# Attention and a gated layer in one kernel: another order at the attention's group boundaries, in its first group, and of the token blocks

## The chip, the cores and the metric

The kernel runs on one core of one Trainium2 chip. The metric is the device time of one execution in microseconds (us), less is better. The engines of a core are PE (matrix products; PEld is its loading of weights, which runs beside the products), DVE (element-wise work), ACT (functions such as tanh and exp), POOL (element-wise work, little used here) and SP (here it issues the transfers). Each engine works through its own list of instructions in order; between engines an instruction waits for semaphores.

## The reference

Attention over 4 batches of 12 heads with 448 tokens of 64 elements, with scores that are capped by a tanh, and then a layer with a cosine gate on the 1792 tokens, all in float32:

```python
scores = cap * np.tanh((q @ k.T / sqrt(64)) / cap)         # per batch and head
scores = scores - scores.max(axis=-1)
attn = np.exp(scores); attn = attn / attn.sum(axis=-1)
x = (attn @ v)                                             # joined over heads: 1792 x 768
h = x @ w_in                                               # 768 -> 2048
return (h * np.cos(h)) @ w_out                             # 2048 -> 768
```

With a cap below a limit, as here, exp needs no maximum and the kernel leaves it out.

## The kernel before, in words

**Attention.** The 48 pairs of a batch and a head are worked in NO = 6 groups of eight; groups n = 0 to 2 hold batches 0 and 1, groups 3 to 5 batches 2 and 3. A group has NC = 7 chunks c of 64 keys, and each chunk two halves a of four pairs. A *unit* j is one half of one chunk: PE computes its scores (`scores`, L293, 8 matmuls into one of two PSUM banks of tag `pair`, each of which the trace shows as two records), and ACT takes the tanh of 128x896 values from the bank into half of a tile `t` (`tanh`, L312). Two units are one *step* (42 in all): ACT then takes exp in place over the whole 128x1792 tile (`exp`, L319). There are four `t` tiles, so the tanh of step i waits until all that reads the tile of step i-4 is done: on DVE the addition of the chunk into the running sum over chunks (`add`, L358, for c = 1 to 5), on PE the product with v (`values`, L376, 16 matmuls of a step into two banks `acc`).

At the end of a group, PE sums over the keys with a matrix of ones, once over the last chunk and once over DVE's running sum (`sums`, L387); the result z takes one of the two `pair` banks too. DVE then makes the result's parts, a chain of nine instructions: transpose (`norm_sums`, L406), reciprocal, transpose, two products of `acc` with the reciprocals into x0 and x1 (`norm_scale`, L423), two copies to the high parts xh (`norm_high`, L428) and two subtractions for the low parts xl (`norm_low`, L431). The first addition of the next group stood behind all nine.

**Order of the work.** `attention` (L448) writes the order out by hand: `at(step, time, call)` puts every call on one list with the key STEP * step + time, and the list is sorted and emitted in that order. Only the order counts; what an engine does first is what comes first on the list. The two weights of 64-bit words are turned into float parts on the way (a *piece* of a weight: one ACT instruction `magnitude`, L197, and six DVE instructions), at the steps of the table DECODE (L37).

**First group.** `unit(j)` (L246) gives the order in which halves and chunks of group 0 are taken: (a, c) = (0,0), (0,1), (1,0), (1,1), (0,2), (0,3), (1,2), (1,3), and then both halves of each chunk. Its chunks 0 and 1 both come due for `values` in step 3, ahead of the scores of step 4.

**The layer.** The tokens are worked in four blocks (BLOCKS, L26), the 2048 hidden columns in 8 groups G of 2x128. One step (`Layers.step`, L679) is one block of one G: PE makes h of both columns (`hidden`, L155, 36 matmuls), then the product with w_out for the block of the step before (`Block.product`, L606, 36 matmuls), while ACT and DVE make the gate. `begin(0)` and `begin(1)` (L649) make h of block 0 already in the attention's last steps. The banks `single` that take h of block 1 are the space that `acc` held, so the first of them waits until `norm_scale` of group 5 has read it.

Of the kernel before, what the change touches and what calls it, by code (L numbers as in the profile page):

```python
# [10 lines left out]
F32 = mybir.dt.float32  # L11
# [3 lines left out]
AF = mybir.ActivationFunctionType  # L15
# [7 lines left out]
DM = H * D  # L23
DFF = 2048
KC = DM // 128
BLOCKS = 512, 512, 384, 384  # L26
STARTS = 0, 512, 1024, 1408
WIDE = max(BLOCKS)
NF = DFF // 128
NQUAD = NPAIR // 2  # L30
# [3 lines left out]
ND = NJ // 2  # L34
DIRECT = 1
STEP = 3.4
DECODE = [(7, 10, 11, 12, 13, 14), (17, 18, 19, 20, 21, 24), (26, 27, 28, 31, 32, 33), (35, 38, 39, 40)]  # L37
BUSY = 8, 3
PAD = 80
QK = 2 * S  # L40
# [204 lines left out]

def unit(j):  # L246
    n, i = divmod(j, 2 * NC)
    if n or i > 7:
        return n, i % 2, i // 2
    return 0, i // 2 % 2, 2 * (i // 4) + i % 2  # L250


WHERE = {unit(j): j for j in range(NJ)}
# [2 lines left out]
class Heads:  # L256


    def __init__(self, ctx, tc, banks, qk, v, capt, inv, xh, xl, bounded):
        nc = tc.nc  # L260
        self.nc, self.qk_in, self.v_in, self.capt, self.inv = nc, qk, v, capt, inv
        if bounded:
            self.inv, self.capt = in_register(nc, inv, "inv"), in_register(nc, capt, "cap")
        self.cap_column = capt
        self.xh, self.xl, self.bounded = xh, xl, bounded
        cp = ctx.enter_context(tc.tile_pool(name="a_const", bufs=1))
        self.ld = ctx.enter_context(tc.tile_pool(name="a_ld", bufs=8 if bounded else 4))
# [8 lines left out]
        self.qk, self.v, self.ps, self.ts, self.left = {}, {}, {}, {}, {}  # L276
        self.sum, self.acc, self.x, self.z, self.r, self.s = {}, {}, {}, {}, {}, {}

    def fill(self):
# [32 lines left out]
    def tanh(self, j):  # L312
        i, k = divmod(j, 2)
        if k == 0:
            self.ts[i] = self.tp.tile([128, 2, 2, S], F32, name="t", tag="t")
            self.left[i] = 2
        self.nc.scalar.activation(self.ts[i][:, k], self.ps.pop(j)[:, :, 0:S], AF.Tanh, scale=self.inv)  # L317

    def exp(self, i):  # L319
        self.nc.scalar.activation(self.ts[i], self.ts[i], AF.Exp, scale=self.capt)  # L320

    def t(self, n, a, c):
        j = WHERE[n, a, c]
        return self.ts[j // 2][:, j % 2]

    def used(self, n, c):
        for a in range(2):
            i = WHERE[n, a, c] // 2
            self.left[i] -= 1
            if not self.left[i]:  # L330
                del self.ts[i]

    def exp_general(self, n):
        nc, ident = self.nc, self.ident
# [112 lines left out]
def attention(ctx, tc, banks, busy, second, qk, v, capt, inv, xh, xl, wts, layers):  # L447
# [7 lines left out]
    def at(step, time, call, *args):  # L455
        todo.append((STEP * step + time, len(todo), call, args))
# [15 lines left out]
    for n in range(NO):  # L472
        begin = NC * n
        for c in range(NC):
            at(begin - 2 * NC + 2 + c if n > 1 else n - 1, 0.3 + 0.1 * c, a.load_v, n, c)
        for p in range(4):
            if n:
                at(begin - NC + (-1, 2, 3, 4)[p] if n > 1 else -0.5, 0.8, a.load, n, p // 2, p % 2)
        for c in range(NC):
            i = max(WHERE[n, p, c] for p in range(2)) // 2 + 2  # L480
            lag = 1 if c < NC - 1 and 0 < n and (n, c) not in ((NO - 1, NC - 3), (NO - 1, NC - 2)) else 0
            if c == NC - 1:
                at(i, 0.3, a.sums, n, c)
                at(i, 0.4, a.sums, n, None)
            for e in range(2):
                at(i + lag, (0.5, 0.7)[e] if c == NC - 1 else 0.1, a.values, n, c, e)
            if 0 < c < NC - 1:
                at(i, 0.15, a.add, n, c)
            if c:
                at(i + lag, 0.75 if c == NC - 1 else 0.18, a.used, n, c)  # L490
            if c == 1:
                at(i + lag, 0.19, a.used, n, 0)
        for m, (part, args) in enumerate([("sums", ()), ("inverse", ()), ("spread", ()), ("scale", (0,)), ("scale", (1,)),
                                          ("high", (0,)), ("high", (1,)), ("low", (0,)), ("low", (1,))]):
            at(i, 1.0 + 0.1 * m, getattr(a, "norm_" + part), n, *args)
    pieces = (("wi", 0), ("wi", 1), ("wo", 0), ("wo", 1), ("wi", 2))
    at(5, 3.3, wts.load, *pieces[0])
    for n, steps in enumerate(DECODE):
# [1 line left out]
                 (wts.high, *pieces[n], nc.vector), (wts.low, *pieces[n], nc.vector)]  # L500
        at(steps[0] - 1, 3.3, wts.magnitude)
        for step, call in zip(steps, calls):
            at(step, 2.5, *call)
        at(steps[3], 2.6, wts.load, *pieces[n + 1])
    at(ND - 1, 1.7, layers.begin, 0)
    at(ND, 1.65, layers.sine)
    at(ND, 1.7, layers.first, second)
    at(ND + 1, 0.3, layers.begin, 1)
    for _, _, call, args in sorted(todo, key=lambda x: x[:2]):
        call(*args)  # L510

# [281 lines left out]
```

## Time and profile before

| | us |
|---|---|
| median of 3 runs (648.32 to 651.06) | 649.91 |
| the profiled execution | 649.24 |
| its span, first to last instruction | 647.4 |
| PE busy in the span | 620.4 (96%) |
| DVE busy | 488.0 (75%) |
| ACT busy | 306.5 (47%) |
| POOL busy | 54.7 (8%) |

The span has two parts with different limits, so its shares are means over both. In the chain of work that ended last, from the span's start to about 185 us PE, ACT and DVE take turns (attention); from there on it is PE alone (the layer). PE's time printed per instruction includes the filling of its pipeline, so neighbouring instructions overlap in the table; from when one starts to when the next starts is the better measure.

### The profile page before, as it was taken

To read this page: it belongs to the slowest core of one execution; us is meant where nothing else is said; L and a number is where in the kernel's file an instruction comes from. 1 tells how busy PE (TensorE), PEld (TensorE's weight loads), DVE (VectorE), ACT (ScalarE), POOL (GpSimd) and SP (SyncE) were. 2 spreads that over 40 slices of the span, in tenths; PEclk is the share of its full clock that TensorE was granted. 3 is DMA by queue.
4 is the path that set the end of the run, shared out by engine and by line. 5 is a ranking of instruction groups with operands and counts; after the bars stand their busy time and mean duration, and the time that the engine had idled before them with its cause. 6 is when DMAs were issued, how large, how long until landed. Compare 5 with 4: busy or idle time off the path is not lost.

```text
span 647.4 us, 11991 instructions
## 1 busy us (share of the span) xinstructions
PE 620.4 (96%) x5207; PEld 470.7 (73%) x5207; DVE 488.0 (75%) x643; ACT 306.5 (47%) x383; POOL 54.7 (8%) x36
## 2 busy tenths in 40 slices
PE   8988898988879999999999999999999999999996
PEld 2323242322458998898899889889988998998896
DVE  1567868778578888777887898788789877877654
ACT  6889897897613343333334333343343333333220
POOL 0000000000011111111111111111111111111000
PEclk9999899999989999999999999999999999999999
DMA  7625243320101112111111221111111221110224
GB/s 230 226 58 177 86 147 121 113 79 2 51 0 51 49 54 94 49 50 50 49 50 50 60 84 52 50 50 49 50 50 49 81 67 49 50 49 1 100 97 152
DMA packets 22782, 48.06 MB, mean 74 GB/s; under 512 B 2496, under 2 KB 9920, under 8 KB 22720
## 3 DMA queue, kind: packets, MB, share of 16 engines
q1 hardware_dynamic: 22576, 47.00, 22.1%
q8 instruction: 43, 0.70, 0.4%
q10 hardware_dynamic: 144, 0.20, 0.1%
q14 instruction: 19, 0.16, 0.1%
HBM read 41.68 MB, written 5.51 MB: 73 GB/s over the span
## 4 chain that ended last, share of the span: by engine, by line
PE 85%; DVE 9%; ACT 4%; issue 1%; DVEq 0%; ACTq 0%
PE single L162 35%; PE pair L619 24%; PE rest L619 12%; PE pair L303 6%; PE acc L381 5%; ACT t L317 2%; DVE x L423 2%; DVE sum L365 2%; DVE xl L431 2%; PE pair L395 1%; PE pair L162 1%; DVE s L406 1%; DVE s L419 1%; ACT t L320 1%; DVE xh L428 1%
## 5 line engine op out<-in xcount | busy, mean ns | idle before, releaser
L582 ACT ACTIVATE y<-y,angles 128x384 f32<-128x384 f32 (+1 forms) x63 | 42.3, 671 | 120.3 <-DVE y L579 120.3
L303 PE MATMUL pair<-qk 64*32 64x448 f32 x1232 | 74.9, 554 | 14.3 <-ACT t L317 14.3
L317 ACT ACTIVATE t<-pair 128x896 f32<-128x896 f32 x84 | 74.3, 935 | 24.1 <-DVE sum L365 16.6
L381 PE MATMUL acc<-t,v 64*32 64x448 f32 x1344 | 77.4, 539 | 0.4 <-DVE x L423 0.2
L320 ACT ACTIVATE t<-t 128x1792 f32<-128x1792 f32 x42 | 72.3, 1725 | 0.0
L632 DVE TENSOR_TENSOR acc<-pair,acc 128x1024 f32<-128x1024 f32 (+1 forms) x56 | 60.8, 1086 | 10.5 <-PE pair L619 10.5
L570 ACT ACTIVATE v<-single,angles 128x384 f32<-128x384 f32 (+1 forms) x62 | 39.1, 630 | 57.2 <-PE single L162 57.1
L303 PEld LDWEIGHTS pair<-qk 64*32 64x32 f32 x1232 | 20.0, 106 | 60.1 <-ACT t L317 47.6
L588 ACT CAST gh<-y 128x384 fp32r<-128x384 f32 (+1 forms) x63 | 35.7, 567 | 51.0 <-DVE y L585 51.0
L381 PEld LDWEIGHTS acc<-t,v 64*32 64x32 f32 x1344 | 26.9, 107 | 40.7 <-issue 29.0
L591 DVE TENSOR_TENSOR gl<-y,gh 128x384 fp32r<-128x384 f32 (+1 forms) x63 | 54.1, 859 | 2.5 <-ACT gh L588 2.5
L197 ACT ACTIVATE u<-w 128x768 f32<-128x768 f32 x32 | 29.2, 912 | 55.1 <-POOL wo2l L230 10.0
L573 DVE TENSOR_SCALAR v<-v 128x384 f32<-128x384 f32 (+1 forms) x63 | 24.6, 390 | 32.4 <-ACT v L570 32.4
L365 DVE TENSOR_TENSOR sum<-sum,t 128x1792 f32<-128x1792 f32 x20 | 40.5, 2025 | 8.8 <-ACT t L320 8.5
L579 DVE SCALAR_TENSOR_TENSOR y<-v,y 128x384 f32<-128x384 f32 (+1 forms) x63 | 39.3, 624 | 2.2
L585 DVE TENSOR_TENSOR y<-single,y 128x384 f32<-128x384 f32 (+1 forms) x62 | 38.3, 617 | 3.2 <-ACT y L582 3.2
L578 DVE SCALAR_TENSOR_TENSOR y<-v,single 128x384 f32<-128x384 f32 (+1 forms) x62 | 38.4, 619 | 2.1
L212 DVE TENSOR_SCALAR u<-u 128x768 f32<-128x768 f32 x32 | 17.7, 554 | 27.7 <-ACT u L197 27.6
L162 PE MATMUL single<-xh,wi0h 128*128 128x384 f32 (+1 forms) x90 | 33.2, 369 | 3.5 <-DVE x L423 3.5
L162 PE MATMUL single<-xh,wi2l 128*128 128x512 f32 (+1 forms) x96 | 35.0, 364 | 0.0
L162 PE MATMUL single<-xh,wi2h 128*128 128x512 f32 (+1 forms) x96 | 34.9, 364 | 0.0
L619 PE MATMUL pair<-gh,wo0l 128*128 128x512 f32 (+1 forms) x96 | 34.8, 363 | 0.0
(153 smaller groups left out, 1461.9 us busy)
## 6 DMA issues: line engine op xcount, KB each, us to landing
w<-in_w_in_dram SPq DMA_DIRECT2D x32, 384.0 KB, 3.6
w<-in_w_out_dram SPq DMA_DIRECT2D x32, 384.0 KB, 3.5
qk<-in_qk_dram SPq DMA_DIRECT2D x20, 448.0 KB, 3.5
v<-in_v_dram SPq DMA_DIRECT2D x42, 128.0 KB, 2.5
out_dram<-acc SPq DMA_DIRECT2D x6, 512.0 KB, 2.7
out_dram<-acc SPq DMA_DIRECT2D x5, 384.0 KB, 3.1
qk<-in_qk_dram SPq DMA_DIRECT2D x2, 288.0 KB, 2.9
qk<-in_qk_dram SPq DMA_DIRECT2D x2, 160.0 KB, 3.6
```

The costliest lines, as they stand in the source:

```text
L162: nc.tensor.matmul(h[:, 0:n], lhsT=w[:, ks], rhs=x[:, k, toks], start=(k == 0 and i == 0), stop=(k == KC - 1 and i == 2))
L303: self.nc.tensor.matmul(ps[o:o + 32, h, 0:S], lhsT=x[mine, k:k + 32], rhs=x[mine, Q], start=True, stop=True, tile_position=(64 * h, o))
L317: self.nc.scalar.activation(self.ts[i][:, k], self.ps.pop(j)[:, :, 0:S], AF.Tanh, scale=self.inv)
L320: self.nc.scalar.activation(self.ts[i], self.ts[i], AF.Exp, scale=self.capt)
L365: self.nc.vector.tensor_add(out, old, self.ts[NC * n + c])
L381: self.nc.tensor.matmul(self.acc[n, e][o, r], lhsT=self.v[n, c][rows, d], rhs=self.t(n, a, c)[rows, h], start=c == 0, stop=c == NC - 1, ti ...
L570: m.nc.scalar.activation(self.v, self.h, AF.Identity, bias=m.quarter, scale=1.0 / (2.0 * math.pi))
L579: m.nc.vector.scalar_tensor_tensor(self.y, self.v, -TWO_PI_LO, self.y, op0=ALU.mult, op1=ALU.add)
L582: self.m.nc.scalar.activation(self.y, self.y, AF.Sin, bias=self.m.half_pi)
L591: self.m.nc.vector.tensor_sub(self.result(1), self.y, self.result(0))
L619: m.nc.tensor.matmul((y[e] if self.last(i) else y[:, e])[:, 0:n], lhsT=w[:, c], rhs=x[:, j, 0:n], start=(j == 0 and k == 0), stop=(j == GF ...
L632: m.nc.vector.tensor_add(acc, y[:, e, 0:n], acc)
```

## The change

Five edits, all of them in the order, apart from the first step's buffers:

1. *At a boundary on DVE*: the first addition of the new group comes right behind the two products `norm_scale`; the two `norm_high` follow it, and the two `norm_low` wait until the end of the new group, ahead of its first transpose.
2. *At a boundary on PE*: both `sums` come ahead of the next group's next eight score matmuls (keys 0.15 and 0.16 in place of 0.3 and 0.4; the scores have 0.2). `begin(1)` moves behind the last `sums` and `values`.
3. *First group*: only the first four units have the other order; the tiles of step 0 are x0 and x1, which are free until the first `norm_scale`, so exp of that step is two instructions of 128x896; `values` of chunks 0 and 1 stand apart, one half of chunk 0 ahead of the scores, the rest between and behind them.
4. *Token blocks*: 512, 384, 512, 384 in place of 512, 512, 384, 384. Block 1 then lies in batches 0 and 1.
5. *Weights and loads*: another table DECODE; loads of v two steps later.

```diff
-BLOCKS = 512, 512, 384, 384
-STARTS = 0, 512, 1024, 1408
+BLOCKS = 512, 384, 512, 384
+STARTS = 0, 512, 896, 1408
...
-DECODE = [(7, 10, 11, 12, 13, 14), (17, 18, 19, 20, 21, 24), (26, 27, 28, 31, 32, 33), (35, 38, 39, 40)]
+DECODE = [(8, 8, 8, 8, 11, 12), (13, 14, 18, 19, 20, 21), (25, 25, 26, 27, 28, 32), (33, 35, 39, 40)]
...
 def unit(j):
     n, i = divmod(j, 2 * NC)
-    if n or i > 7:
+    if n or i > 3:
         return n, i % 2, i // 2
-    return 0, i // 2 % 2, 2 * (i // 4) + i % 2
+    return 0, i // 2, i % 2
...
         if k == 0:
-            self.ts[i] = self.tp.tile([128, 2, 2, S], F32, name="t", tag="t")
+            if i or not self.bounded:
+                t = self.ts[i] = self.tp.tile([128, 2, 2, S], F32, name="t", tag="t")
+                self.half[i] = [t[:, 0], t[:, 1]]
+            else:
+                self.half[i] = [self.np.tile([128, 2, S], F32, name=f"x{e}", tag=f"x{e}") for e in range(2)]
...
-        self.nc.scalar.activation(self.ts[i], self.ts[i], AF.Exp, scale=self.capt)
+        for t in [self.ts[i]] if i else self.half[i]:
+            self.nc.scalar.activation(t, t, AF.Exp, scale=self.capt)
...
-            at(begin - 2 * NC + 2 + c if n > 1 else n - 1, 0.3 + 0.1 * c, a.load_v, n, c)
+            at(begin - 2 * NC + 4 + c if n > 1 else n - 1, 0.3 + 0.1 * c, a.load_v, n, c)
...
             if c == NC - 1:
-                at(i, 0.3, a.sums, n, c)
-                at(i, 0.4, a.sums, n, None)
+                at(i, 0.15, a.sums, n, c)
+                at(i, 0.16, a.sums, n, None)
             for e in range(2):
-                at(i + lag, (0.5, 0.7)[e] if c == NC - 1 else 0.1, a.values, n, c, e)
+                time = (0.5, 0.7) if c == NC - 1 else (0.1, 2.0) if i == 3 and c == 0 else (2.5, 2.51) if i == 3 else (0.1, 0.1)
+                at(i + lag, time[e], a.values, n, c, e)
...
-        for m, (part, args) in enumerate([("sums", ()), ("inverse", ()), ("spread", ()), ("scale", (0,)), ("scale", (1,)),
-                                          ("high", (0,)), ("high", (1,)), ("low", (0,)), ("low", (1,))]):
+        for m, (part, args) in enumerate([("sums", ()), ("inverse", ()), ("spread", ()), ("scale", (0,)), ("scale", (1,))]):
             at(i, 1.0 + 0.1 * m, getattr(a, "norm_" + part), n, *args)
+        for e in range(2):
+            at(i + 2, 0.5, a.norm_high, n, e)
+            at(i + NC if n < NO - 1 else i + 2, 0.9, a.norm_low, n, e)
...
-    at(ND + 1, 0.3, layers.begin, 1)
+    at(ND + 1, 0.9, layers.begin, 1)
```

DVE at the boundary from group 3 to group 4, before (`u`, `wo0h` are a weight's pieces, `s` and `r` the reciprocals on their way, `sum` the running sum):

```order
L218 SCALAR_TENSOR_TENSOR u<-w_77,u 128x768
L406 STREAM_TRANSPOSE s<-pair 128x896
L413 RECIPROCAL r<-s 128x28
L419 STREAM_TRANSPOSE s<-r 128x896
L423 TENSOR_TENSOR x_1572<-acc,s 128x896
L423 TENSOR_TENSOR x_1574<-acc,s 128x896
L428 CAST xh<-x_1572 128x896
L428 CAST xh<-x_1574 128x896
L431 TENSOR_TENSOR xl<-x_1572,xh 128x896
L431 TENSOR_TENSOR xl<-x_1574,xh 128x896
L365 TENSOR_TENSOR sum<-t 128x1792
```

The same place on DVE now (lines are numbered anew; L371 is the addition, L412 the first transpose, L437 the low parts):

```order
L215 TENSOR_SCALAR u<-u 128x768
L437 TENSOR_TENSOR xl<-x_1240,xh 128x896
L437 TENSOR_TENSOR xl<-x_1242,xh 128x896
L412 STREAM_TRANSPOSE s<-pair 128x896
L419 RECIPROCAL r<-s 128x28
L425 STREAM_TRANSPOSE s<-r 128x896
L429 TENSOR_TENSOR x_1574<-acc,s 128x896
L429 TENSOR_TENSOR x_1576<-acc,s 128x896
L371 TENSOR_TENSOR sum<-t 128x1792
L434 CAST xh<-x_1574 128x896
L434 CAST xh<-x_1576 128x896
```

The addition has moved up past four instructions; the low parts that stand ahead of the transpose are those of the group before, x_1240 and x_1242.

PE at a boundary before (L303 scores, L395 sums, L381 values):

```order
L381 MATMUL acc<-t,v 32x448 x16
L303 MATMUL pair<-qk 32x448 x8
L395 MATMUL pair<-t,one 32x448 x8
L395 MATMUL pair<-sum,one 32x448 x8
L381 MATMUL acc<-t,v 32x448 x8
L303 MATMUL pair<-qk 32x448 x8
```

PE at a boundary now (L401 sums, L387 values):

```order
L387 MATMUL acc<-t,v 32x448 x16
L401 MATMUL pair<-t,one 32x448 x8
L401 MATMUL pair<-sum,one 32x448 x8
L303 MATMUL pair<-qk 32x448 x8
L387 MATMUL acc<-t,v 32x448 x8
L303 MATMUL pair<-qk 32x448 x8
```

Sums and the first eight scores have changed places. z so takes the `pair` bank ahead of them, and the second eight scores get the bank that z held.

DVE at the end of attention, before (`second` is the gate of the layer's first unit):

```order
L579 SCALAR_TENSOR_TENSOR second<-second 128x512
L585 TENSOR_TENSOR second<-pair,second 128x512
L406 STREAM_TRANSPOSE s<-pair 128x896
L413 RECIPROCAL r<-s 128x28
L419 STREAM_TRANSPOSE s<-r 128x896
```

And now:

```order
L588 SCALAR_TENSOR_TENSOR second<-second 128x512
L594 TENSOR_TENSOR second<-pair,second 128x512
L437 TENSOR_TENSOR xl<-x_1892,xh 128x896
L437 TENSOR_TENSOR xl<-x_1894,xh 128x896
L412 STREAM_TRANSPOSE s<-pair 128x896
```

Here too the two low parts of the group before have come in between the gate and the last group's chain.

## Rows read from the trace of the kernel before

**Rows 1.** Windows: length, busy (count) of PE, PEld, DVE, ACT, POOL; clock, DMA, GB/s

```profile
6.85:49.31 42.46, 38.27 (x700) 13.00 (x684) 20.79 (x22) 35.22 (x34) 0.00 (x0) 1.00 0.54 175
49.31:157.73 108.42, 98.55 (x1920) 34.30 (x1920) 82.89 (x75) 93.42 (x87) 0.00 (x0) 0.98 0.34 108
185.45:189.08 3.63, 3.63 (x10) 2.80 (x11) 3.02 (x4) 0.52 (x1) 0.00 (x0) 0.57 0.00 0
303.39:361.19 57.80, 57.80 (x289) 52.06 (x289) 47.75 (x68) 21.09 (x33) 7.39 (x4) 1.00 0.17 55
```

**Rows 2.** Waits of ACT, 5 to 170 us: total, times, longest

```profile
ACT t L317 <- DVE sum L365: 16.6, 5, 3.5
ACT t L317 <- PE pair L303: 7.5, 10, 2.8
```

**Rows 3.** Waits of PE's weight loads, 5 to 170 us

```profile
PEld pair L303 <- ACT t L317: 49.1, 53, 2.8
```

**Rows 4.** ACT timeline, boundary of groups 3 and 4: start, length, ..., [idle before <-releaser]

```profile
125.39 1.70 ACT L320 ACTIVATE t<-t 128x1792 f32<-128x1792 f32 x1
130.47 1.73 ACT L317 ACTIVATE t<-pair 128x896 f32<-128x896 f32 x2 [3.38 <-DVE sum L365]
...
133.67 1.73 ACT L317 ACTIVATE t<-pair 128x896 f32<-128x896 f32 x2
```

**Rows 5.** DVE timeline, the same boundary

```profile
113.87 2.02 DVE L365 TENSOR_TENSOR sum<-sum,t 128x1792 f32<-128x1792 f32 x1 [0.70 <-ACT t L320]
115.82 0.99 DVE L218 SCALAR_TENSOR_TENSOR u<-w,u 128x768 int32<-128x768 int32 x1
120.55 1.12 DVE L406 STREAM_TRANSPOSE s<-pair 128x896 f32<-128x896 f32 x1 [3.74 <-PE pair L395]
...
123.28 2.09 DVE L423 TENSOR_TENSOR x<-acc,s 128x896 f32<-128x896 f32 x2
125.28 1.16 DVE L428 CAST xh<-x 128x896 fp32r<-128x896 f32 x2
126.35 2.09 DVE L431 TENSOR_TENSOR xl<-x,xh 128x896 fp32r<-128x896 f32 x2
128.35 2.02 DVE L365 TENSOR_TENSOR sum<-t 128x1792 f32<-128x1792 f32 x1
```

**Rows 6.** PE timeline, the same boundary

```profile
118.71 0.99 PE L395 MATMUL pair<-t,one 64*32 64x448 f32 x16
119.48 0.96 PE L395 MATMUL pair<-sum,one 64*32 64x448 f32 x16
...
126.20 1.71 PE L303 MATMUL pair<-qk 64*32 64x448 f32 x32
127.70 1.72 PE L381 MATMUL acc<-t,v 64*32 64x448 f32 x32
```

**Rows 7.** ACT timeline, first group

```profile
19.89 1.73 ACT L317 ACTIVATE t<-pair 128x896 f32<-128x896 f32 x2 [0.96 <-PE pair L303]
...
27.36 1.73 ACT L317 ACTIVATE t<-pair 128x896 f32<-128x896 f32 x2 [0.96 <-PE pair L303]
```

**Rows 8.** DVE timeline, end of attention

```profile
174.44 0.69 DVE L585 TENSOR_TENSOR second<-pair,second 128x512 f32<-128x512 f32 x1 [0.79 <-ACT second L582]
180.58 1.12 DVE L406 STREAM_TRANSPOSE s<-pair 128x896 f32<-128x896 f32 x1 [5.45 <-PE pair L395]
```

**Rows 9.** PE timeline, end of attention

```profile
179.49 0.98 PE L395 MATMUL pair<-sum,one 64*32 64x448 f32 x16
...
185.45 0.50 PE L162 MATMUL single<-xh,wi0h 128*128 128x512 f32 x1 [3.48 <-DVE x L423]
```

**Rows 10.** ACT timeline, the layer's first step

```profile
195.16 0.62 ACT L588 CAST gh<-y 128x512 fp32r<-128x512 f32 x1 [0.76 <-DVE y L585]
```

**Rows 11.** Chain that ended last, one turn of the layer: start, length, what

```profile
303.39 8.20 PE single L162 x36
...
319.75 6.26 PE single L162 x36
```

More of the change, by code (lines that the diff above doesn't have):

```diff
@@ L275, in __init__ @@
             make_identity(nc, self.ident)
-        self.qk, self.v, self.ps, self.ts, self.left = {}, {}, {}, {}, {}
+        self.qk, self.v, self.ps, self.ts, self.half, self.left = {}, {}, {}, {}, {}, {}
         self.sum, self.acc, self.x, self.z, self.r, self.s = {}, {}, {}, {}, {}, {}
@@ L314, in tanh @@
         if k == 0:
-            self.ts[i] = self.tp.tile([128, 2, 2, S], F32, name="t", tag="t")
+            if i or not self.bounded:
[3 more added lines that the diff above has]
+                self.half[i] = [self.np.tile([128, 2, S], F32, name=f"x{e}", tag=f"x{e}") for e in range(2)]
             self.left[i] = 2
-        self.nc.scalar.activation(self.ts[i][:, k], self.ps.pop(j)[:, :, 0:S], AF.Tanh, scale=self.inv)
+        self.nc.scalar.activation(self.half[i][k], self.ps.pop(j)[:, :, 0:S], AF.Tanh, scale=self.inv)
     def exp(self, i):
-        self.nc.scalar.activation(self.ts[i], self.ts[i], AF.Exp, scale=self.capt)
+        for t in [self.ts[i]] if i else self.half[i]:
+            self.nc.scalar.activation(t, t, AF.Exp, scale=self.capt)
     def t(self, n, a, c):
         j = WHERE[n, a, c]
-        return self.ts[j // 2][:, j % 2]
+        return self.half[j // 2][j % 2]
     def used(self, n, c):
@@ L330, in used @@
             if not self.left[i]:
-                del self.ts[i]
+                self.ts.pop(i, None)
+                del self.half[i]
     def exp_general(self, n):
@@ L489, in attention @@
             if c:
-                at(i + lag, 0.75 if c == NC - 1 else 0.18, a.used, n, c)
+                at(i + lag, 0.75 if c == NC - 1 else 2.6 if i == 3 else 0.18, a.used, n, c)
             if c == 1:
-                at(i + lag, 0.19, a.used, n, 0)
-        for m, (part, args) in enumerate([("sums", ()), ("inverse", ()), ("spread", ()), ("scale", (0,)), ("scale", (1,)),
-                                          ("high", (0,)), ("high", (1,)), ("low", (0,)), ("low", (1,))]):
+                at(i + lag, 2.61 if i == 3 else 0.19, a.used, n, 0)
+        for m, (part, args) in enumerate([("sums", ()), ("inverse", ()), ("spread", ()), ("scale", (0,)), ("scale", (1,))]):
             at(i, 1.0 + 0.1 * m, getattr(a, "norm_" + part), n, *args)
+        for e in range(2):
+            at(i + 2, 0.5, a.norm_high, n, e)
+            at(i + NC if n < NO - 1 else i + 2, 0.9, a.norm_low, n, e)
     pieces = (("wi", 0), ("wi", 1), ("wo", 0), ("wo", 1), ("wi", 2))
@@ L502, in attention @@
         for step, call in zip(steps, calls):
-            at(step, 2.5, *call)
+            at(step, 0.6 if step == 8 else 2.5, *call)
         at(steps[3], 2.6, wts.load, *pieces[n + 1])
```

## The prediction

> **What bounds the kernel now.** I read the windows by stage first, then the waits of the engine that is fullest in each, then the timelines around the longest of these waits, and last the chain that ended last.
>
> The windows split the span. One turn of the layer (a group G over four blocks) takes 57.80 us and PE is busy in all of them [rows 1]: there PE sets the time, and only columns taken away would shorten it. Attention is different. The second row of [rows 1] runs from the tanh that ended the wait at the first boundary to the one that ended the wait at the last, four whole groups: 108.42 us, with ACT busy in 93.42, PE in 98.55, DVE in 82.89. No engine is full, so something makes them take turns. ACT's waits name it [rows 2]: 16.6 us in five waits of up to 3.5 us for a DVE addition, against 7.5 us in ten waits for scores. PE waits for ACT in turn, 53 times [rows 3], so it is not what holds ACT up in general. How long a step takes undisturbed is read off the starts: 130.47 to 133.67, 3.20 us on ACT [rows 4]; PE starts the scores of a step at 126.20 and its values at 127.70 [rows 6], so 1.50 for each part and 3.00 for a step. Attention wants to run at ACT's pace, 3.2 us a step, with about 0.2 to spare on PE.
>
> The timeline of one boundary shows why it doesn't. ACT ends an exp at about 127.1 and idles 3.38 us until 130.47 [rows 4], because the next tanh needs the tile that the first addition of the new group still reads. On DVE the addition runs from 128.35 for 2.02 us, and before it from 120.55 stand the nine instructions that make the result's parts [rows 5]. The four of them that nobody waits for, the copies and the subtractions, take 125.28 to 128.35, 3.07 us.
>
> **The addition moved ahead (edit 1).** It now starts behind the two products, at what was 125.28, 3.07 us sooner, and the 3.38 us of ACT's idle time shrink to 0.3. Five boundaries, 16.6 us [rows 2]. The copies follow behind the addition, where DVE otherwise waits for the next exp (0.70 us idle before 113.87 alone [rows 5]); DVE has 108.42 - 82.89 = 25.5 us idle in four groups, 6.4 a group, and its work doesn't grow. The subtractions (2.09 us for two) go into the hole of 3.74 us that DVE has ahead of the first transpose [rows 5]. That cover is thin, so I lay it out. The last addition starts at 113.87 and ends at 115.9; a weight's instruction of up to 0.99 and the subtractions of 2.09 end at 118.9.
>
> **Sums ahead of eight scores (edit 2).** The two sums start 0.77 us apart [rows 6], eight scores take half of 1.50; so z is ready about 0.75 us sooner and the transpose can start at about 119.8 instead of 120.55: 0.9 us behind the subtractions. The whole chain and the addition move up by those 0.75 us too, and the rest of ACT's wait, 0.3, is covered. What it costs: the eight scores come later by the two sums, 1.5 us, and the second eight get the bank of z, which is free only after the transpose (1.12 us [rows 5]), beside which PE has eight `values` (0.75) to do. No row shows ACT in this order. The bounds are 0, where ACT still has a tanh and an exp ahead of it, and the full 1.5 us of the sums; no row is nearer to one end, so I take 0.7 a boundary.
>
> For the four groups of the window: ACT's idle time is 108.42 - 93.42 = 15.0 [rows 1], which holds four boundary waits and the small waits for scores; 4 x 0.7 = 2.8 stays. **Gain 12.2**, bounds 9.0 (4 x 1.5 stays) and 15.0.
>
> **First group (edit 3).** Its window is 42.46 us with ACT busy 35.22, so 7.2 idle [rows 1]: the fifth boundary wait (3.4), two holes of 0.96 in front of scores [rows 7], and smaller ones. The first hole comes where 3.0 us of values of two chunks stand ahead of the next scores; with only one half of chunk 0 there (0.75) it goes. The rest of these values then stands ahead of the next step's scores, and since PE has only 0.2 a step to spare I expect some 0.8 of it back one step later, plus 0.7 at the boundary and 0.5 of small ones: 2.0 stay. The exp in two parts costs nothing that counts: its two halves need ACT no longer than the two tanh of a step do, of the same size, 1.73 together against 1.70 for one exp [rows 4]. **Gain 5.2**, bounds 3.4 (the boundary alone) and 6.6.
>
> **End of attention (edits 1, 2 and 4).** The last transpose waits until 180.58 for the last sums, which stand behind `begin(1)` and start at 179.49 [rows 8, 9]. Now the sums come first, and the transpose waits for DVE: the gate ends at 175.13 [rows 8], the two subtractions that were put ahead of it end at 177.2. The chain starts 3.4 us sooner, and with it the moment at which the banks of `acc` come free and PE goes on, 185.45 before [rows 9]. Not all of it stays. The first product of the layer needs the copy that ACT ends at 195.78 [rows 10], 10.3 us after PE's restart, and this distance runs over DVE and ACT and doesn't change: the product starts near 192.4. But h of block 1 is now 384 wide, 6.26 in place of 8.20 us for 36 matmuls [rows 11], so PE comes to that point early and waits; the 1.94 us of columns are not saved, they come later, in block 2. **Gain 3.4 - 1.9 = 1.5**, bounds 0 and 3.4.
>
> PE's clock belongs here. After its idle 3.48 us the granted clock was 0.57 for the next 3.63 us, so mostly the lower of 1.2 and 2.4 GHz, and ten matmuls took 3.63 in place of 2.28 us (8.20 / 36 each) [rows 1, 9, 11]: 1.35 lost. In the new order PE idles twice for 2 to 3 us there. The Trainium skill (TensorE: Matmul & The Clock Gate, What's actually happening) says that the low clock is the default state and that activity releases it. By that rule the second wait could lose what the first did, and the gain at this place would be 0.1; without it, 1.5. The trace agrees that idling is followed by the low clock. I take 1.5 and keep 0 as the bound.
>
> **Token blocks in the layer (edit 4): nothing.** A turn has the same 72 x 1792 columns in either order, and PE is full [rows 1]. What could break this is a gate that comes late: between h of a 512 block and its product PE now has the 384 block's h and the product of a 384 block, 2 x 6.26 = 12.5 us, where it was 6.26 + 8.20 = 14.5 [rows 11]. In the first step ACT and DVE needed 10.3 us for all that stood between, weights included. DVE is busy 47.75 of 57.80 [rows 1]. It fits.
>
> **Weights and loads (edit 5): nothing.** As many instructions, placed where DVE waits; the later loads of v still stand over ten steps (32 us) ahead of their use.
>
> **Sum.** 12.2 + 5.2 + 1.5 = 18.9. The profiled execution took 649.24, so 630.3; the median of the runs is 0.67 higher. I say 630.5. Its own bounds: 649.24 - 25.0 = 624.2 and 649.24 - 12.4 = 636.8.
>
> **Rivals.**
>
> *PE is nearer to full than its starts say.* By busy time PE could not go below 98.55 in the four groups and 38.27 in the first [rows 1]: gains 9.9 and 4.2, with 1.5 at the end 15.6, time 633.6. Against it: starts 1.50 apart while 1.71 is printed [rows 6], and PE's waits for ACT [rows 3]. The Trainium skill (Perfetto Trace Analysis, Identifying the Most-Contended Engine) says that matmul busy time is no good measure here and the load of weights is better; PEld is busy 34.30 of 108.42 [rows 1], which agrees. Chance 0.10.
>
> *The wait moves to z.* The 0.9 us between subtractions and transpose are used up as ACT gets faster, DVE's chain starts late, and the second eight scores, which need z's bank, with it. Each microsecond late passes to ACT. With 1.9 late at five boundaries half of the gain is gone: about 640. For it: DVE is busy 82.89 of what would now be 96, 86%. Chance 0.14.
>
> *The same idle time, elsewhere.* If another reader of the tile (the values of chunk 0, behind the products' release of `acc`) ended as late as the addition did, only the first group and the end would gain, at best 3.3 and at worst nothing: 646 to 650. Against it: PE starts values at 127.70 of the second chunk already while ACT waits [rows 6]. Chance 0.05.
>
> *Slower.* The same place as with z, decided by how late: the new order is slower once the chain starts more than about 4 us late at a boundary (3.3 saved, and 6.7 / 5 gained elsewhere, less the 0.7). It would need the low parts and weights to push DVE from 118.9 to 124. At 5 us it is 5 x (5 + 0.7 - 3.3) - 6.7 = 5.3 slower, 654.5. Against it: 6.4 us of DVE's time a group are idle. Chance 0.05.
>
> **How the numbers follow.** Forecast 0.66, the rivals 0.10, 0.14, 0.05 and 0.05. The range takes the forecast's own bounds and most of the z case: 624 to 638.5. About 0.5% (3.2 us) is what a measurement here can tell from no change; the first three cases lie below it: faster 0.90, same 0.05, slower 0.05.
>
> **What would show it.** Right: no wait of ACT for an addition over 0.5 us; the four groups in about 96 us; ACT's waits below 6 us in all; PE restarting behind attention about 3.4 us nearer to the last exp's end; turns of the layer still at 57.8. Wrong: boundary waits of ACT now put down to scores, with DVE's transpose right behind subtractions without a hole, or turns above 58.

## The result, and the profile after

| | before | after |
|---|---|---|
| median, same chip (4 runs each) | 650.00 us (648.32 to 651.06) | 629.86 us (629.20 to 630.14) |
| the profiled execution / its span | 649.24 / 647.4 us | 629.20 / 627.4 us |
| PE busy in the span | 620.4 us (96%) | 612.8 us (98%) |

The ratio is 0.9691, with a 95% interval of 0.9668 to 0.9713. 630.5 had been forecast, so 0.64 less than that came out. The span has lost 20.0 us, against a sum of 18.9. Windows of the kernel after, cut at the same events as [rows 1] (first group, four groups, PE's restart behind attention, one turn of the layer; columns as there):

```profile
6.81:44.08 37.27, 34.82 (x667) 13.07 (x660) 20.79 (x22) 35.06 (x35) 0.00 (x0) 1.00 0.69 228
44.08:139.70 95.62, 93.74 (x1931) 34.19 (x1921) 81.32 (x73) 93.23 (x89) 0.00 (x0) 1.00 0.35 111
164.30:168.00 3.70, 3.58 (x12) 3.58 (x13) 3.14 (x5) 0.47 (x1) 0.00 (x0) 0.55 0.00 0
298.40:356.20 57.80, 57.80 (x290) 52.09 (x289) 46.81 (x70) 21.19 (x32) 7.30 (x5) 1.00 0.16 55
```

The first group takes 37.27 in place of 42.46, the four groups 95.62 in place of 108.42; ACT is busy as long as before (93.23, 93.42) and now fills 98% of that stretch. PE's restart still comes at the low clock. The fourth window was cut as long as the old turn, so its 57.80 is not a measurement; the chain that ended last has the same h of two turns start 57.80 us apart before (303.39 in [rows 11] and 361.19) and 57.74 apart now:

```profile
298.34 8.16 PE single L162 x36
356.08 8.16 PE single L162 x36
```

The whole span falls into pieces, each from one event to the next. (The product in the last two rows is the layer's first with the columns of `wo1h`; it starts at 196.06 before, where PE does not wait for it, and at 174.81 now.)

| piece of the span | before | after | gain | forecast |
|---|---|---|---|---|
| start to first tanh | 6.85 | 6.81 | 0.04 | 0 |
| first group | 42.46 | 37.27 | 5.19 | 5.2 |
| four groups | 108.42 | 95.62 | 12.80 | 12.2 |
| to the end of the last exp | 11.30 | 11.29 | 0.01 | 0 |
| last exp's end to that product of the layer | 27.03 | 23.82 | 3.21 | 3.4 |
| from that product to the end | 451.34 | 452.59 | -1.25 | -1.9 |

Waits of ACT in the kernel after, 5 to 170 us (total, times, longest), where [rows 2] had 16.6 us for additions:

```profile
ACT v L579 <- PE pair L162: 5.7, 1, 5.7
ACT t L321 <- PE pair L303: 4.5, 12, 0.8
ACT wo1h L448 <- DVE xl L437: 4.3, 1, 4.3
```

Among its tanh and exp there is no wait for an addition left. What is left of them waits for scores, 4.5 us in twelve pieces, and 2.8 us more in which the very first tanh waits; [rows 2] had that wait among its 7.5, and now it is listed apart, since the tile of step 0 is an x. (The first and third row lie behind the last exp, in the layer's gate.) The boundary of groups 3 and 4 on ACT, to be read against [rows 4]:

```profile
106.64 1.77 ACT L325 ACTIVATE t<-t 128x1792 f32<-128x1792 f32 x1
108.67 0.92 ACT L321 ACTIVATE t<-pair 128x896 f32<-128x896 f32 x1 [0.25 <-PE pair L303]
109.48 1.69 ACT L325 ACTIVATE t<-t 128x1792 f32<-128x1792 f32 x1
111.07 1.71 ACT L321 ACTIVATE t<-pair 128x896 f32<-128x896 f32 x2
113.12 0.92 ACT L321 ACTIVATE t<-pair 128x896 f32<-128x896 f32 x1 [0.33 <-PE pair L303]
```

The 3.38 us have become 0.25 and 0.33. And on DVE, against [rows 5]:

```profile
102.04 2.03 DVE L371 TENSOR_TENSOR sum<-sum,t 128x1792 f32<-128x1792 f32 x1 [0.29 <-ACT t L325]
103.98 0.56 DVE L450 CAST wo0h<-u 128x768 fp32r<-128x768 f32 x1
104.45 2.09 DVE L437 TENSOR_TENSOR xl<-x,xh 128x896 fp32r<-128x896 f32 x2
107.91 1.12 DVE L412 STREAM_TRANSPOSE s<-pair 128x896 f32<-128x896 f32 x1 [1.37 <-PE pair L401]
110.64 2.09 DVE L429 TENSOR_TENSOR x<-acc,s 128x896 f32<-128x896 f32 x2
112.65 2.02 DVE L371 TENSOR_TENSOR sum<-t 128x1792 f32<-128x1792 f32 x1
114.58 1.16 DVE L434 CAST xh<-x 128x896 fp32r<-128x896 f32 x2
```

The subtractions lie in the hole ahead of the transpose and leave 1.37 us of it, where 0.9 had been worked out; at the other three boundaries of the window it is 1.18, 1.37 and 1.53. The addition follows the products at once. At the end of attention, on DVE and on PE, against [rows 8, 9]:

```profile
156.94 0.69 DVE L594 TENSOR_TENSOR second<-pair,second 128x512 f32<-128x512 f32 x1 [0.79 <-ACT second L591]
157.55 2.08 DVE L437 TENSOR_TENSOR xl<-x,xh 128x896 fp32r<-128x896 f32 x2
159.55 1.11 DVE L412 STREAM_TRANSPOSE s<-pair 128x896 f32<-128x896 f32 x1
```

```profile
164.42 0.47 PE L162 MATMUL single<-xh,wi0h 128*128 128x384 f32 x1 [1.93 <-DVE x L429]
...
174.81 0.50 PE L628 MATMUL pair<-gh,wo1h 128*128 128x512 f32 x1 [1.61 <-ACT gh L597]
```

Here the transpose has no hole: it starts the moment the two subtractions end. PE waits 1.93 us for the products and later, its narrower h of block 1 done, 1.61 us for ACT's copy.

### The profile page after: what moved, and what is told of

Same layout as the page of the kernel before. It is cut to its first block, busy times and chain, and to the rows that moved or that the text cites. A ratio compares the mean times of both kernels' runs of the same rounds, so it can differ in the third digit from the quotient of the medians.

```text
span 627.4 us, 11992 instructions
## 1 busy us (share of the span) xinstructions
PE 612.8 (98%) x5206; PEld 472.0 (75%) x5207; DVE 485.7 (77%) x643; ACT 306.3 (49%) x384; POOL 55.3 (9%) x36
## 4 chain that ended last, share of the span: by engine, by line
PE 90%; ACT 6%; DVE 3%; issue 0%; DMA 0%; DVEq 0%; ACTq 0%
PE single L162 34%; PE pair L628 25%; PE rest L628 12%; PE pair L303 8%; PE acc L387 7%; ACT t L321 3%; ACT t L325 2%; PE pair L401 1%; PE pair L162 1%; PE idle L63 1%; DVE xl L437 1%; PE acc L63 0%; PE single L628 0%; DVE x L429 0%; DVE gl L600 0%
## 5 line engine op out<-in xcount | busy, mean ns | idle before, releaser
L321 ACT ACTIVATE t<-pair 128x896 f32<-128x896 f32 x82 | 72.3, 939 | 4.6 <-PE pair L303 4.5
L387 PE MATMUL acc<-t,v 64*32 64x448 f32 x1312 | 72.9, 536 | 0.0
L303 PE MATMUL pair<-qk 64*32 64x448 f32 x1232 | 70.0, 540 | 2.5 <-ACT t L321 2.0
L325 ACT ACTIVATE t<-t 128x1792 f32<-128x1792 f32 x41 | 70.7, 1728 | 0.0
L303 PEld LDWEIGHTS pair<-qk 64*32 64x32 f32 x1232 | 20.8, 106 | 43.9 <-ACT t L321 20.2
L600 DVE TENSOR_TENSOR gl<-y,gh 128x384 fp32r<-128x384 f32 (+1 forms) x63 | 51.9, 823 | 2.5 <-ACT gh L597 2.5
L387 PEld LDWEIGHTS acc<-t,v 64*32 64x32 f32 x1312 | 26.2, 107 | 34.9 <-issue 33.0
L371 DVE TENSOR_TENSOR sum<-sum,t 128x1792 f32<-128x1792 f32 x20 | 40.5, 2025 | 9.8 <-ACT t L325 9.8
L628 PE MATMUL pair<-gl,wo0h 128*128 128x512 f32 (+1 forms) x96 | 34.8, 363 | 0.0
L628 PE MATMUL pair<-gh,wo0h 128*128 128x512 f32 (+1 forms) x96 | 34.8, 363 | 0.0
```

What stands on the lines that cost most here:

```text
L303: self.nc.tensor.matmul(ps[o:o + 32, h, 0:S], lhsT=x[mine, k:k + 32], rhs=x[mine, Q], start=True, stop=True, tile_position=(64 * h, o))
L321: self.nc.scalar.activation(self.half[i][k], self.ps.pop(j)[:, :, 0:S], AF.Tanh, scale=self.inv)
L325: self.nc.scalar.activation(t, t, AF.Exp, scale=self.capt)
L371: self.nc.vector.tensor_add(out, old, self.ts[NC * n + c])
L387: self.nc.tensor.matmul(self.acc[n, e][o, r], lhsT=self.v[n, c][rows, d], rhs=self.t(n, a, c)[rows, h], start=c == 0, stop=c == NC - 1, ti ...
L600: self.m.nc.vector.tensor_sub(self.result(1), self.y, self.result(0))
```

## The experiments

There are two theories of where the 20 us come from. The first is that of the forecast: DVE's order removes the boundary waits, the sums ahead of scores gain a little more, the first group two microseconds of its own, and the 384-wide block only costs. The rival was that one edit does nearly all of it (sums first alone could take the chain out of ACT's way), so that the sum came out for the wrong reason. Four kernels do one edit each, on one chip, and none does edit 5 by itself; before had 650.07 us (19 runs, 648.49 to 653.90) beside them.

**Edit 1 alone.** The order of `high` and `low` of the change, nothing else:

```diff
-        for m, (part, args) in enumerate([("sums", ()), ("inverse", ()), ("spread", ()), ("scale", (0,)), ("scale", (1,)),
-                                          ("high", (0,)), ("high", (1,)), ("low", (0,)), ("low", (1,))]):
+        for m, (part, args) in enumerate([("sums", ()), ("inverse", ()), ("spread", ()), ("scale", (0,)), ("scale", (1,))]):
...
+        for e in range(2):
+            at(i + 2, 0.5, a.norm_high, n, e)
+            at(i + NC if n < NO - 1 else i + 2, 0.9, a.norm_low, n, e)
```

> Only edit 1 on DVE (addition ahead of the copies, subtractions at the end of the next group). Theory (the addition behind four instructions that nobody waits for was the boundary wait): five waits of 3.3 us shrink to about 0.3 us, about 15 us faster, 635 us; the end of attention gains nothing, since the last sums still stand behind begin(1). Rival (the gain needs the sums ahead of the scores as well, because the transposes wait for them): less than half, 643 us or more.

Measured 635.99 (635.15 to 636.46), ratio 0.9762 [0.9716, 0.9808]. ACT waits for additions twice, 0.8 us in all. First tanh to the last exp's end took 146.9 in place of 162.2. Of these 15.3 us the end gave 2.1 back: from the last exp's end to the layer's first product it is 29.14, not 27.03. PE waits there 1.75 us and then 3.48 us, as it did before, but now the clock falls behind both and not only behind the second. The first of these waits in before and here, and the window from 1.1 us after the second row's start:

```profile
175.18 0.50 PE L162 MATMUL pair<-xh,wi1h 128*128 128x512 f32 x1 [1.75 <-DVE second L585]
```

```profile
160.43 0.50 PE L162 MATMUL pair<-xh,wi1h 128*128 128x512 f32 x1 [1.75 <-DVE second L587]
```

```profile
161.50:165.70 4.20, 4.20 (x13) 3.30 (x12) 0.88 (x1) 0.00 (x0) 0.00 (x0) 0.59 0.01 4
```

The eighteen matmuls behind this wait, ahead of the last sums, take 5.92 us from the first one's start to the sums' in place of 4.31, so 1.6 of the 2.1 are the clock. In attention edit 1 is the largest by far, as forecast.

**Edit 2 alone.**

```diff
-                at(i, 0.3, a.sums, n, c)
-                at(i, 0.4, a.sums, n, None)
+                at(i, 0.15, a.sums, n, c)
+                at(i, 0.16, a.sums, n, None)
...
-    at(ND + 1, 0.3, layers.begin, 1)
+    at(ND + 1, 0.9, layers.begin, 1)
```

> Only edit 2 on PE (sums ahead of eight scores, begin(1) behind the last sums). Theory: at the boundaries the chain starts 0.75 us sooner and ACT's wait shrinks by as much at most, less 0.3 us of new waits for scores; at the end of attention the last chain starts 5.4 us sooner, since no subtractions stand ahead of it: 5 to 9 us faster, 641 to 645 us. Rival (the end of attention is not on the path, PE waits for the layer's first copies anyway): 647 us or more.

Measured 638.74 (638.66 to 638.84), ratio 0.9806 [0.9761, 0.9852]: more than expected. Its waits of ACT:

```profile
ACT t L317 <- DVE sum L365: 10.9, 5, 2.3
ACT t L317 <- PE pair L303: 8.6, 13, 3.5
```

The additions hold ACT up for 10.9 us in place of 16.6, about 1.1 a boundary. Attention gained 5.3, 0.7 to 1.1 a group, and 1.1 more in one group that ran partly at the low clock before (0.94 in its window). The larger half is at the end, 5.8: with the sums ahead of `begin(1)` and no subtractions in the way, the distance from the last exp to the product is 21.26. The sizes of edits 1 and 2 don't add up (14.1 + 11.3 is more than the whole 20): both shorten the same boundary waits, and edit 1 brings group 4's subtractions ahead of the last chain, where they take back a part of those 5.8. No one edit does nearly all of the 20 us: it is 14.1 with edit 1 and 11.3 with edit 2.

**Edit 3 alone** (order of the first units, half tiles, times of `values`, later loads of v):

```diff
-    if n or i > 7:
+    if n or i > 3:
...
+                time = (0.5, 0.7) if c == NC - 1 else (0.1, 2.0) if i == 3 and c == 0 else (2.5, 2.51) if i == 3 else (0.1, 0.1)
+                at(i + lag, time[e], a.values, n, c, e)
```

> Only edit 3 (order of the first group, its buffers and the later loads of v). Theory: the two holes of 0.96 us on ACT give way to one of about 0.8 us: 1 to 2 us faster, 648 to 649 us; the five boundary waits stay at 3.0 to 3.5 us. Rival (the later loads of v or the exp in two parts cost): 650 us or more.

Measured 649.64 (647.61 to 651.20), ratio 0.9983 [0.9960, 1.0006]: by the time, inconclusive. The trace is clearer: from the first tanh to that of step 11 it takes 40.61 us in place of 42.46, 1.85 less; the boundary waits stay (16.6 us in five). One hole of 0.81 us is where two of 0.96 were [rows 7], which makes 1.1 of the 1.85. Most of the rest is two other waits of ACT that became shorter: for a weight's transfer, ahead of `magnitude` (0.49 for 0.94), and ahead of the second tanh (0.34 for 0.65).

**Edit 4's blocks alone.**

```diff
-BLOCKS = 512, 512, 384, 384
-STARTS = 0, 512, 1024, 1408
+BLOCKS = 512, 384, 512, 384
+STARTS = 0, 512, 896, 1408
```

> Only the token blocks 512, 384, 512, 384. Theory: the turns of the layer stay at 57.8 us, and at its start the 1.94 us of columns that block 1 has less are work taken out of the time that PE waits in anyway, and done later: about 1.9 us slower, 652 us. Rival (no wait there, or the shorter block frees something): 650 us or less.

Measured 651.67 (649.46 to 652.88) beside the 650.07 of before, ratio 1.0000 [0.9976, 1.0023]: inconclusive by the time too. The wait that the forecast named is there in its trace:

```profile
198.29 0.50 PE L619 MATMUL pair<-gh,wo1h 128*128 128x512 f32 x1 [1.87 <-ACT gh L588]
```

**The change with the old blocks.** What the noise of before hides should be seen on the quieter kernel after. The first of these ran on another chip than after, so it was done again beside a second run of after.

```diff
-BLOCKS = 512, 384, 512, 384
-STARTS = 0, 512, 896, 1408
+BLOCKS = 512, 512, 384, 384
+STARTS = 0, 512, 1024, 1408
```

> The changed kernel with the token blocks of before (512, 512, 384, 384). Theory: PE waits 2.6 us for the layer's first copies in the changed kernel; with 512 columns in block 1 it does 1.9 us more work in that time, which is then not there later: about 1.9 us faster than the changed kernel, 628 us. Rival (block 1 of 512 waits for the last group's parts, which it then needs): not faster, 630 us or more.

Measured 628.72 (628.33 to 629.38), ratio 0.9651 [0.9630, 0.9673].

> The changed kernel once more, on the chip of this call, for comparison with the others: 629 to 630 us.

> The changed kernel with the token blocks of before, again, beside the changed kernel on one chip. Theory (the block order costs the time that PE waits in for the first copies): 1.1 to 1.9 us faster than the changed kernel. Rival (the first comparison was one of chips): the same within 0.5 us.

Measured on one chip: the change as it is 630.02 (six runs, 629.56 to 632.70), with the old blocks 628.45 (628.00 to 628.86); all five of these lie below all six. So the new blocks cost about 1.6 us. The wait is 1.6 us too, and not the 2.6 that the first expectation names. PE's two rows say why. With the new blocks, and then with the old:

```profile
174.66 0.50 PE L628 MATMUL pair<-gh,wo1h 128*128 128x512 f32 x1 [1.60 <-ACT gh L597]
```

```profile
174.91 0.39 PE L628 MATMUL pair<-gh,wo1h 128*128 128x512 f32 x1
```

With the new blocks ACT's copy sets when the product starts, 10.37 us behind PE's restart. With the old blocks PE has 512 columns of h to do first, comes to the product 0.2 us later (10.57) and waits for nothing; with the new ones it has done 384 and does the rest later.

**Group 4's subtractions out of the last chain's way.** They go three steps ahead, where DVE waits:

```diff
-            at(i + NC if n < NO - 1 else i + 2, 0.9, a.norm_low, n, e)
+            at(i + NC - 3 if n == NO - 2 else i + NC if n < NO - 1 else i + 2, 0.9, a.norm_low, n, e)
```

> The changed kernel with the two subtractions of group 4 three steps earlier, in a hole of DVE, so that they no longer stand between the gate and the last chain. Theory: the last chain, PE's restart and the layer's first product all come 2.0 us sooner: 628 us, PE's wait for norm_scale nearly gone. Rival (the chain hangs on the last sums or values, not on DVE): no change, 630 us.

Measured 629.75 (627.66 to 629.94), ratio 0.9654 [0.9630, 0.9678]: almost nothing gained. The chain did move. The last exp's end to the product is 21.79 in place of 23.82, so the subtractions had cost 2.0 us there, and PE restarts without a wait at full clock. But the rest of the layer takes 454.76 us in place of 452.59. (Up to DVE's last addition, without the transfer of the result, whose length differs from run to run, it is 448.91 in place of 447.37, 1.5 more.) The product that waits, and the windows behind the restart and behind this wait:

```profile
173.24 0.49 PE L628 MATMUL pair<-gh,wo1h 128*128 128x512 f32 x1 [3.18 <-ACT gh L597]
```

```profile
162.64:166.64 4.00, 4.00 (x24) 3.79 (x23) 3.23 (x5) 1.38 (x2) 0.00 (x0) 1.00 0.00 0
173.24:177.24 4.00, 4.00 (x10) 2.89 (x11) 3.17 (x6) 1.80 (x3) 0.00 (x0) 0.59 0.00 0
```

PE now runs through h sooner and at the full clock, so it comes to the product earlier and waits longer, 3.18 us, and the granted clock falls to 0.59 behind that wait: ten matmuls in 4 us. Most of the 2.0 us gained ahead of the product is lost behind it. The five runs say the same: the one with a mean granted clock of 1.000 took 627.66, the three at 0.993 to 0.994 took 629.75 to 629.94. That reading was tested by itself.

**The same with work in the wait.** Twelve matmuls whose result nobody reads stand ahead of the first product; all else is as in the run before:

```diff
+        if step == 1:
+            keep_busy(nc, self.banks.rest()[:, 0], self.warm, 12)
```

> As b2_low4_early, with twelve idle matmuls of 128x512 on zeros (about 2.6 us) between h of block 1 and the layer's first product, where PE waited 3.2 us and its granted clock then was 0.59 for 4 us; their result is not used. Theory (b2 gave back its 2.0 us because PE's clock fell behind the longer wait): the clock stays at 1.0 there, the product starts as soon as in b2, and the time is 627.5 to 628 us with little spread. Rival (the 2 us were lost elsewhere in the layer): 629.5 to 630 us, as b2.

Measured 627.76 (627.16 to 628.01), ratio 0.9643 [0.9620, 0.9666]. That is 2.3 less than the change on the same chip (630.02), and 2.0 less than the run before, which was on another chip. The window behind the product:

```profile
173.00:177.00 4.00, 3.95 (x16) 2.98 (x17) 3.76 (x7) 1.80 (x3) 0.00 (x0) 1.00 0.01 4
```

Sixteen matmuls in 4 us at full clock. From the product to DVE's last addition it is 447.36, as in the change (447.35 on this chip), so the clock was all that the run before had lost there.

**Both: early subtractions and old blocks.** Here the 512-wide h fills most of the wait with work that has to be done anyway.

> Both of these together. Theory: the two add up, about 3.9 us faster than the changed kernel, 626 us. Rival (one wait covers both): 628 us, as either alone.

Measured 626.50 (625.42 to 626.98), ratio 0.9613 [0.9591, 0.9635]: the fastest of all, 3.4 below the 629.86 of the change. Its wait at the product is 1.22 us, with the clock at 1.00 behind it.

**The rival "the wait moves to z", priced.** Four groups' subtractions are done twice, ahead of the transpose, the second time with the same operands, so that the chain starts late by a known amount.

```diff
+            if n < NO - 2:
+                at(i + NC, 0.85, a.norm_low_again, n, e)
```

> The changed kernel with the two subtractions done twice at the first four boundaries where they stand ahead of the transpose (2.0 us of DVE more at each, same result). Theory: the hole of 1.2 to 1.5 us ahead of the transpose covers most; the remaining 0.5 to 0.8 us pass to ACT through the bank that z holds, 2 to 3 us slower than the changed kernel, 632 to 633 us. Rival (the chain is not on ACT's path by then, since the addition ends before ACT needs the tile): no change, 630 us; rival (all of it passes): 8 us, 638 us.

Measured 631.50 (631.38 to 632.31), ratio 0.9697 [0.9676, 0.9719]. Counted from the start of the second sum, the transposes start 1.62 to 1.98 us behind it in place of 1.06 to 1.25: 0.4 to 0.7 late each, 2.2 in all. The four groups show 0.7 of it, 96.34 for 95.62: a third passes to ACT. The rest of the difference is the clock again, 0.60 behind the product, though PE had waited only 1.60 us for it: from there to DVE's last addition it is 448.97 in place of 447.37. The time lies a little below what the theory expected.

**Three times instead of twice.**

```diff
+            if n < NO - 2:
+                at(i + NC, 0.85, a.norm_low_again, n, e)
+                at(i + NC, 0.86, a.norm_low_again, n, e)
```

> The changed kernel with the two subtractions done three times at four boundaries (4.0 us of DVE more at each, same result), so that the transpose starts about 2.6 us late. b4_more_before_transpose had it 0.5 to 0.8 us late at each and lost 0.7 us in all in these groups. Theory (ACT has about 0.9 us to spare between the end of the addition and its next tanh, after which all passes on): about 1.7 us a boundary, 6 to 7 us slower, 636 to 637 us. Rival (all of the lateness passes through the bank of z): 10 us, 640 us. Rival (a third passes, as in b4): 3 us, 633 us.

Measured 645.59 (644.95 to 646.00), ratio 0.9918 [0.9890, 0.9945]: a clear miss, some 9 us above what was expected. The first of these boundaries on DVE, on PE and on ACT, and the windows behind it:

```profile
57.51 4.09 DVE L437 TENSOR_TENSOR xl<-x,xh 128x896 fp32r<-128x896 f32 x4
61.52 2.09 DVE L440 TENSOR_TENSOR xl<-x,xh 128x896 fp32r<-128x896 f32 x2
63.52 1.11 DVE L412 STREAM_TRANSPOSE s<-pair 128x896 f32<-128x896 f32 x1
...
68.03 1.09 DVE L429 TENSOR_TENSOR x<-acc,s 128x896 f32<-128x896 f32 x1 [0.69 <-PE acc L387]
```

```profile
59.90 0.96 PE L401 MATMUL pair<-sum,one 64*32 64x448 f32 x16
...
61.40 0.96 PE L387 MATMUL acc<-t,v 64*32 64x448 f32 x16
64.69 1.75 PE L303 MATMUL pair<-qk 64*32 64x448 f32 x16 [2.32 <-DVE s L412]
66.18 1.74 PE L387 MATMUL acc<-t,v 64*32 64x448 f32 x16
```

```profile
66.54 0.92 ACT L321 ACTIVATE t<-pair 128x896 f32<-128x896 f32 x1 [2.32 <-PE pair L303]
68.96 1.73 ACT L321 ACTIVATE t<-pair 128x896 f32<-128x896 f32 x2 [1.50 <-PE pair L303]
```

```profile
64.00:68.00 4.00, 3.31 (x40) 1.11 (x48) 3.16 (x4) 1.14 (x2) 0.00 (x0) 0.59 0.04 16
68.00:88.00 20.00, 20.00 (x432) 7.21 (x424) 18.53 (x16) 19.04 (x18) 0.00 (x0) 1.00 0.44 136
```

The transpose starts 3.62 us behind the second sum (59.90 to 63.52), 2.6 late; at the others it is 2.4 to 2.8. The second eight scores wait 2.32 us for z's bank. That alone would cost ACT 2.3 less what it has in hand. Three things come on top. The granted clock falls to 0.59, and eight scores need 1.49 us from start to start (64.69 to 66.18) in place of 0.75. `values` of the last chunk stand behind those scores on PE's list, so the second product on DVE waits 0.69 us for them. And ACT waits a second time, 1.50 us. At the four boundaries these pairs of waits make 2.32 + 1.50, 2.71 + 1.64, 1.55 + 0.58 and 1.95 + 2.00, in all 14.25, where the change has about 0.6 each. The third pair is a control that the run has in itself: the second scores waited 2.32 us there too, but the clock stayed at 1.00 behind it.

```profile
119.68 0.99 PE L303 MATMUL pair<-qk 64*32 64x448 f32 x16 [2.32 <-DVE s L412]
```

```profile
120.77 0.92 ACT L321 ACTIVATE t<-pair 128x896 f32<-128x896 f32 x1 [1.55 <-PE pair L303]
122.27 1.73 ACT L321 ACTIVATE t<-pair 128x896 f32<-128x896 f32 x2 [0.58 <-PE pair L303]
```

At that price, 2.13, four boundaries would have cost 6 us more than in the change, as the theory said; the other three took 3.82 to 4.35 each, and there the clock fell. A further 2.4 us lie behind the layer's first product (449.76 to DVE's last addition), where PE had waited 3.17 us and the clock was 0.50.

## Why the prediction was right

*What bounds attention.* Right. ACT's pace, 3.2 us a step, is what the four groups now run at: 28 steps of it would be 89.6, 95.62 it is, and 93.23 of that is ACT's busy time.

*The addition moved ahead, and sums ahead of scores.* Right in the mechanism, and the sum of the two is 12.80 for 12.2. 0.7 of waiting was left for each boundary, a choice near the middle of 0 and 1.5 that no row supported; ACT's rows show 0.25 + 0.33. The 15.0 us of idle time that it started from held about 1.1 us that are no wait of this kind: in the profiled execution of before the clock fell behind one boundary (the group of 0.94), which the forecast doesn't name. Edit 1 alone (ACT's waits for additions 0.8 us for 16.6) and edit 2 alone, worth some 0.8 a boundary (0.75 was the term), show both terms apart. The cover of the subtractions was worked out too thin by 0.3 to 0.6 us.

*First group.* 5.19 for 5.2, with the hole that stays of 0.81 for 0.8. Edit 3 alone gave 1.85 of it, with the boundary wait left in; the forecast's own split (7.2 idle less the boundary's 3.4 and the 2.0 that stay) gives 1.8. The exp in two parts costs 0.09 us (1.68 from start to start for 1.59).

*Weights and loads: nothing.* Not quite. Among the "smaller ones" of the first group was ACT's wait for a weight's transfer, which the forecast didn't name. With the piece a step later it is gone; before and after:

```profile
31.61 0.96 ACT L197 ACTIVATE u<-w 128x768 f32<-128x768 f32 x1 [0.94 <-DMA v<-in_v_dram]
```

```profile
32.62 0.93 ACT L197 ACTIVATE u<-w 128x768 f32<-128x768 f32 x1
```

Edit 3 with its later loads of v left 0.49 of this wait, so about half of the 0.94 seems to be the table's; no run shows the table by itself.

*End of attention.* Net 1.96 for 1.5. The chain started 2.99 us nearer to the last exp's end (159.55 less 150.99, against 180.58 less 169.03), 3.4 had been said; PE's restart likewise. The stretch behind the product is 1.25 longer, for 1.94. So the gain was put 0.2 to 0.4 too high and the cost 0.7 too high, and that the two errors partly cancel is luck. Why the cost is lower can be read off the chain: up to DVE's last addition the stretch is 1.43 longer (445.94 to 447.37), and the seven turns of the kernel after, each 0.067 shorter than before, give back 0.47 of the 1.94. The last 0.2 lies behind that addition, in the transfer of the result.

*PE's clock at the end.* PE waited twice, as said, though 1.93 and 1.61 us and not 2 to 3. Behind the first the granted clock was 0.55, behind the second 1.00. The fall behind the first is on nobody's path: PE waits for ACT's copy right afterwards, and in the run with the early subtractions, where it restarts at full clock, the product comes at the same distance from the restart (10.39 us in both). The fall that costs is one behind the product, and there the 1.5 had no row to go by. It was partly luck: of the six further runs of the change four took 629.56 to 630.03 (mean clock 0.996 to 0.999) and two 632.40 and 632.70 (0.993). No trace of these two was kept, so where their clock fell is not shown. The Trainium skill (TensorE: Matmul & The Clock Gate, What's actually happening) calls the throttled state the default and says that activity releases it; the run with twelve matmuls in the wait agrees (0.59 became 1.00, and the 1.5 us behind the product came back). By that rule alone the second wait of the kernel after was in danger as much as the first; in its trace it kept its clock.

*Token blocks "in the layer: nothing".* Right within 0.07 us a turn, 57.73 (the mean of seven) for 57.80. Taken with the end of attention the new blocks cost 1.6 us: what they bring in the turns, 0.47, is less than what they cost at the layer's start.

*Rivals.* "PE is nearer to full" is refuted: the four groups take 95.62 us, less than the 98.55 that PE was busy in them. "The same idle time, elsewhere" is refuted by the waits. "The wait moves to z" did not come about, since the holes of 1.2 to 1.5 us remain. (At the first boundary a weight's instructions run up to the transpose; ACT waits 0.36 and 0.25 us there.) Its price was wrong on both sides. A microsecond of lateness was to pass to ACT in full: of 0.4 to 0.7 us a third passes, and of 2.6 us more than all, because of the clock and of what stands behind the waiting scores on PE's list. The slower case was to begin at about 4 us late; at 2.6 late, at four boundaries, 5.2 of the 20.8 us are left (645.59 against 630.02 for the change and 650.79 for before, on one chip). The change itself stands 1.2 us of hole away from the first lateness.

*The signs.* No wait for an addition, 95.62 us in the four groups and the length of the turns came as said. ACT's waits among tanh and exp are below the 6 us that were named (4.5) only without the first tanh's 2.8, which was there before too. PE's restart is 2.99 us nearer, for 3.4.

What stays open: why the clock falls behind some waits and not behind others of the same length (1.61 us without, 1.60 us with), and why a turn is 0.067 us shorter in the new order of blocks.

## What to carry to other kernels

Look for instructions that nobody waits for in front of one that somebody waits for, on an engine that works its list in order; move them to where that engine waits anyway, and read the length of that hole first, since past its end the price may climb faster than one to one. An edit that is good at four places can be bad at the fifth: the subtractions that fit the hole ahead of the transpose at four boundaries had none at the end of attention, and put the chain off by 2.0 us there. When PE gets through sooner and waits longer, look at the granted clock behind the new wait before counting the gain; useful columns in that wait (the old blocks, 626.50) were worth more than idle matmuls (627.76, on another chip; two runs of one kernel on these two chips gave 628.72 and 628.45).

## What the runs showed of the hardware

The granted clock behind a wait of PE was not a matter of the wait's length alone. Over the 4 us behind it, it fell to between 0.50 and 0.69, so mostly to the lower of 1.2 and 2.4 GHz, behind waits of 1.60, 1.75, 1.93, 2.03, 2.32, 2.73, 3.17, 3.18 and 3.48 us. It stayed at 1.00 behind others, among them ones of 1.22, 1.26, 1.60, 1.61, 1.75, 1.87, 1.92, 2.03 and 2.32 us. The boundary waits of before, 2.03 us on PE, show both in one trace. The clock fell behind one of the five, where the 32 records print 3.24 us, and not behind the next:

```profile
76.62 3.24 PE L303 MATMUL pair<-qk 64*32 64x448 f32 x32 [2.03 <-ACT t L317]
104.27 1.79 PE L303 MATMUL pair<-qk 64*32 64x448 f32 x32 [2.03 <-ACT t L317]
```

In the run with the other blocks alone it fell behind four of the five.

Behind the layer's first product a fall cost 1.6 us with the subtractions done twice and 1.5 with the early subtractions, counted up to DVE's last addition against the change (448.97 and 448.91 for 447.37). In the runs of before time and clock go together: beside the experiments of one edit each they reach from 648.49 us at a mean granted clock of 0.997 to 653.90 at 0.979. The change has none of those boundary waits, and its runs lie closer together (629.20 to 630.14 beside the 648.32 to 651.06 of before), but for the two at 632.40 and 632.70.
